# A dynamic convolution feeding a squared-ReLU FFN: fixed instruction order, FFN matmuls in groups of six chunks, one PSUM ring

## The chip, the cores and the metric

The kernel runs on one core of a Trainium2 chip. The metric is device time in microseconds (us) for one execution, lower is better. Engine names in the profile: PE is the matrix engine, PEld its weight loads, DVE the vector engine, ACT the scalar (activation) engine, POOL the GpSimd engine, SP the engine that only issues DMAs here.

## The reference

Each token has 192 channels in 8 heads of 24, and for each head seven softmax weights. The first stage replaces every channel by the weighted sum of itself and its six predecessors in time; the second is a two-layer FFN with hidden width 2048 and a squared ReLU. There are 8 batches of 4096 tokens.

```python
w = softmax(weight_gen, axis=-1)                  # (8, 4096, 8 heads, 7 taps)
x_pad = concat([zeros((B, 6, 192)), x], axis=1)   # causal
# y[b,s,h,g] = sum_k w[b,s,h,k] * x_pad[b, s+k, h, g]
y = einsum('bshk,bskhg->bshg', w, windows(x_pad)).reshape(B*S, 192)
h = maximum(y @ w_in, 0)                          # w_in  (192, 2048)
out = (h * h) @ w_out                             # w_out (2048, 192)
```

## The kernel before

The 32768 tokens are worked in 64 blocks of `TB = 512`, eight blocks to a batch. All matrix work is in 16-bit floats with 32-bit sums in PSUM.

**Softmax** (`st_wg_load`, `st_softmax`). Per batch: one load of the raw weights into a tile of 128 partitions with 32 rows of time and a halo of 6 (38 rows x 8 heads x 7 taps = 2128 numbers), one `Exp` on ACT, one sum and one reciprocal on DVE, and five multiplications on DVE (L147, four of 448 numbers and one of 336) that write the scaled weights, skewed, into a buffer `v`. That buffer goes to DRAM as `vd`, from which blocks read their rows. The weights of batch b+1 are loaded at the first block of batch b, and their softmax stands in the text at its third block.

**Block preparation.** `st_load(j)` reads the block's rows of `vd` (tile `wr`, through the SP queue) and of `x` (tile `xt`, through the POOL queue, cast to 16 bits). `st_band` (five a block, on DVE) multiplies `wr` by a 0/1 band mask into `bd`, a banded matrix for each head. `st_conv(j)` runs 80 small matmuls `xt`, `bd` into the PSUM tile `yp`: each uses 32 columns of the array, and four such column strips work side by side. `st_y_evac(j)` copies `yp` to the 16-bit tile `y` on DVE (L241).

**FFN.** The hidden width is 16 chunks of 128 and is worked in eight pairs `fp`. The 192 input channels are 128 + 64, so `st_mm1` issues, for a pair, two matmuls with `w_a` over 128 rows (L249) and two with `w_b` over 64 rows (L262); the latter two use the upper and the lower half of the array's rows, side by side. All four have 512 columns and write `h`, a PSUM tile of two banks. `st_relu` (ACT, L273) turns `h` into `t`, `st_sq` (DVE, L279) squares it into `g`. `st_mm2(j, part)` is chunk by chunk of tokens: a part is eight matmuls of 192 columns (L289) for 128 tokens and half of the hidden chunks; after four parts ACT copies the PSUM tile `o` to `o_sb` (L298) and SP writes it out. `st_mm2` works on the block before, so each of the eight slots of block j holds the first product of one pair of block j and eight matmuls of the second product of block j-1.

PSUM has eight banks: one tile `yp` (two banks), two tiles `h` (four), two tiles `o` (one each). The order in which each engine gets its instructions is not the text's: a planner sorts them by its own estimate of costs, with the text order as priority. Each engine then runs its list in order.

Of the kernel before, what the change touches and what calls it, by code (L numbers as in the profile page):

```python
# [6 lines left out]

ROW_TILED = True
# [3 lines left out]
def kernel(  # L12
# [16 lines left out]
    nc = tc.nc  # L29
    f32 = mybir.dt.float32  # L30
# [17 lines left out]
    RH = R + KK - 1  # L48
# [33 lines left out]
    vbuf = [const.tile([P, RH + KK - 1, H, SL], f16, name=f"v{i}") for i in range(2)]  # L82
# [13 lines left out]
    def load_weights():  # L96
        nc.gpsimd.dma_start(out=w_a, in_=moe_w_in[0:P, :])
        nc.gpsimd.dma_start(out=w_b[0:LO, :], in_=moe_w_in[P:D, :])
        if ROW_TILED:
            nc.gpsimd.dma_start(out=w_b[LO:P, :], in_=moe_w_in[P:D, :])  # L100
        else:
            nc.vector.memset(w_b[LO:P, :], 0.0)
        nc.gpsimd.dma_start(out=w_o, in_=moe_w_out.rearrange("(c p) m -> p c m", p=P))


    wg_t, vd_t = {}, {}

    def st_wg_load(b):
        wg = p_wg.tile([P, RH, H, KK], f32, name="wg")
        wg_t[b] = wg  # L110
        base = weight_gen[b, 0:R]
        if b < B - 1:
            src = bass.AP(
                tensor=base.tensor, offset=base.offset,
                ap=[[R * HK, P], [1, RH * HK]],
            )
            nc.sync.dma_start(out=wg.rearrange("p r h k -> p (r h k)"), in_=src)
        else:
            nc.vector.memset(wg[:, R:RH], 0.0)
            nc.sync.dma_start(  # L120
                out=wg[:, 0:R].rearrange("p r h k -> p (r h k)"),
                in_=weight_gen[b].rearrange("(p r) h k -> p (r h k)", p=P),
            )
            src = bass.AP(
                tensor=base.tensor, offset=base.offset + R * HK,
                ap=[[R * HK, P - 1], [1, (KK - 1) * HK]],
            )
            nc.sync.dma_start(
                out=wg[0 : P - 1, R:RH].rearrange("p r h k -> p (r h k)"), in_=src
            )  # L130

    def st_softmax(b):
        wg = wg_t[b]
        v = vbuf[b % 2]
        nc.scalar.activation(out=wg, in_=wg, func=ActF.Exp)  # L135
        ssum = p_sm.tile([P, RH, H], f32, name="ssum")
        nc.vector.tensor_reduce(out=ssum, in_=wg, axis=AxisX, op=AluOp.add)  # L137
        rcp = p_sm.tile([P, RH, H], f32, name="rcp")
        nc.vector.reciprocal(out=rcp, in_=ssum)  # L139
        pp = list(v.ap[0])  # L140
        for i0 in range(0, RH, SL):
            n = min(SL, RH - i0)
            vo = bass.AP(
                tensor=v.tensor, offset=v.offset + i0 * H * SL,
                ap=[pp, [H * SL + 1, n], [SL, H], [H * SL, KK]],
            )
            nc.vector.tensor_tensor(  # L147
                out=vo,
                in0=wg[:, i0 : i0 + n],
                in1=rcp[:, i0 : i0 + n].unsqueeze(-1).broadcast_to((P, n, H, KK)),  # L150
                op=AluOp.mult,
            )
        vd = p_dr.tile([S, H * SL], f16, name="vd")
        vd_t[b] = vd
        nc.sync.dma_start(
            out=vd.rearrange("(p r) c -> p (r c)", p=P),
            in_=v[:, KK - 1 : KK - 1 + R].rearrange("p r h c -> p (r h c)"),
        )
# [56 lines left out]
    def st_conv(j):  # L215
        yp = ps_y.tile([P, 2, TB], f32, name="yp")
# [21 lines left out]
    def st_y_evac(j):  # L238
        y = p_y.tile([P, 2, TB], f16, name="y")
        y_t[j] = y  # L240
        nc.vector.tensor_copy(out=y, in_=yp_t[j])  # L241

    def st_mm1(j, fp):
        y = y_t[j]
        h = ps_h.tile([P, 2, TB], f32, name="h")
        h_t[(j, fp)] = h
        for jj in range(2):
            fc = 2 * fp + jj
            nc.tensor.matmul(  # L249
                out=h[:, jj, :], lhsT=w_a[:, fc * P : (fc + 1) * P], rhs=y[:, 0, :],  # L250
                start=True, stop=False,
            )
            if not ROW_TILED:
                nc.tensor.matmul(
                    out=h[:, jj, :], lhsT=w_b[:, fc * P : (fc + 1) * P], rhs=y[:, 1, :],
                    start=False, stop=True,
                )
        if ROW_TILED:
            for jj in range(2):
# [3 lines left out]
                    out=h[:, jj, :],  # L263
# [11 lines left out]
    def st_sq(j, fp):  # L275
        if fp == 0:
            g_t[j] = p_g.tile([P, NF, TB], f16, name="g")
        t1 = t1_t[(j, fp)]
        nc.vector.tensor_tensor(  # L279
            out=g_t[j][:, 2 * fp : 2 * fp + 2, :], in0=t1, in1=t1, op=AluOp.mult  # L280
        )

    def st_mm2(j, part):
        c, half = part // 2, part % 2
        if part % 4 == 0:
            o_t[(j, c // 2)] = ps_o.tile([P, 2, Dm], f32, name="o")
        o = o_t[(j, c // 2)]
        for fc in range(half * NF // 2, (half + 1) * NF // 2):
            nc.tensor.matmul(  # L289
                out=o[:, c % 2, :],  # L290
                lhsT=g_t[j][:, fc, c * P : (c + 1) * P],
                rhs=w_o[:, fc, :],
                start=(fc == 0), stop=(fc == NF - 1),
            )
        if part % 4 == 3:
            hf = c // 2
            o_sb = p_os.tile([P, 2, Dm], f32, name="o_sb")
            nc.scalar.copy(out=o_sb, in_=o)  # L298
            g0 = j * TB + hf * 2 * P
            nc.sync.dma_start(  # L300
                out=out[g0 : g0 + 2 * P, :].rearrange("(s p) d -> p s d", p=P),
                in_=o_sb,
            )

    with nc.allow_low_precision("fp16 matmul pipeline"):
        st_wg_load(0)
        for v in vbuf:
            nc.vector.memset(v, 0.0)  # L308
# [3 lines left out]
        st_softmax(0)  # L312
        st_load(0)
        load_weights()
        st_load(1)
        st_load(2)
# [4 lines left out]
        for j in range(NBLK + 1):  # L321
            nb = j // NBB + 1
            if j < NBLK and nb < B:
                if j % NBB == 0:
                    st_wg_load(nb)
                if j % NBB == 2:
                    st_softmax(nb)
            if j + 3 < NBLK:
                st_load(j + 3)
            for fp in range(NFP):  # L330
                if j < NBLK:
                    st_mm1(j, fp)
                    st_relu(j, fp)
                if j >= 1:
                    st_mm2(j - 1, fp)
# [38 lines left out]
```

## Time and profile before

| | us |
|---|---|
| median of three runs | 957.94 (957.47 to 959.33) |
| the profiled execution, its own time | 957.37 |
| its span, first to last instruction | 955.7 |
| PE busy / DVE / ACT / POOL | 863.3 / 686.6 / 587.3 / 64.9 |
| mean granted PE clock | 0.975 of full |

The span is cut into 40 slices in the profile's second part (23.9 us each; a digit is a tenth). Matmul durations in the profile are from the first column in to the last result out, so that consecutive ones overlap; the distance between their starts is what they cost in a row. A group's row gives busy time, mean duration of one, and the idle time ahead of it with what ended it.

### The profile page before, as it was taken

The page shows a single profiled execution, that of the slowest core. Times are in us where ns is not written, and L with a number is a line of the kernel's source. Part 1 is how long each engine was busy: PE and PEld are TensorE (multiplying, and loading weights), DVE is VectorE, ACT ScalarE, POOL GpSimd, SP SyncE. Part 2 cuts the span into 40 slices and gives each one's busy share as a digit, 9 for nine tenths or more (in the row PEclk, how much of TensorE's full clock was granted, in tenths as well). Part 3 has the DMA queues.
Part 4 walks back from the last instruction along what each step waited for, and adds up shares of the span by engine and source line. Part 5 has one row for each costly group of instructions (what it writes and reads, how often), then busy time and mean ns, then how long its engine had stood idle before and what let it go on. Part 6 is the DMA issues. An engine that isn't in the chain of part 4 may idle for free.

```text
span 955.7 us, 25454 instructions
## 1 busy us (share of the span) xinstructions
PE 863.3 (90%) x11264; PEld 504.9 (53%) x11264; DVE 686.6 (72%) x955; ACT 587.3 (61%) x649; POOL 64.9 (7%) x98
## 2 busy tenths in 40 slices
PE   0195847799999999999999999999999999999998
PEld 0043423455555555555555555555555555555555
DVE  7799997986666666666676666766667666676653
ACT  2173625467666676666766667666676666766665
POOL 4000000000000000000000000000000000000000
PEclk9998777799999999999999999999999999999999
DMA  9533433233332233332333323333233322333011
GB/s 209 153 51 92 114 76 113 62 66 62 54 62 50 54 62 54 61 51 53 62 54 60 52 52 62 54 60 52 53 62 54 60 49 56 61 55 55 27 34 43
DMA packets 123950, 62.52 MB, mean 65 GB/s; under 512 B 88641, under 2 KB 121536, under 8 KB 122944
## 3 DMA queue, kind: packets, MB, share of 16 engines
q0 software_dynamic: 44480, 17.57, 16.7%
q1 hardware_dynamic: 79360, 43.33, 15.8%
q8 instruction: 88, 1.44, 0.6%
q14 instruction: 22, 0.18, 0.1%
HBM read 49.09 MB, written 29.36 MB: 82 GB/s over the span
## 4 chain that ended last, share of the span: by engine, by line
PE 79%; DVE 16%; DMA 3%; issue 1%; ACT 1%; SPq 0%; ACTq 0%; DVEq 0%
PE o L289 37%; PE h L249 21%; PE h L262 15%; DVE v L147 8%; PE yp L228 6%; DVE g L279 3%; DMA wg<-in_weight_gen_dram 2%; DVE bd L200 2%; DVE rcp L139 1%; DVE ssum L137 1%; DVE y L241 1%; DMA wr<-vd 1%; ACT t L273 0%; DMA vd<-v 0%; ACT wg L135 0%
## 5 line engine op out<-in xcount | busy, mean ns | idle before, releaser
L273 ACT ACTIVATE t<-h 128x1024 f16<-128x1024 f32 x512 | 523.3, 1023 | 303.1 <-PE h L262 283.1
L279 DVE TENSOR_TENSOR g<-t 128x1024 f16<-128x1024 f16 x512 | 353.3, 693 | 245.2 <-ACT t L273 242.6
L289 PE MATMUL o<-w_o,g 128*128 128x192 f16 x4096 | 430.0, 249 | 0.3 <-DVE g L279 0.2
L289 PEld LDWEIGHTS <-g 128*128 128x128 f16 x4096 | 314.9, 98 | 117.0 <-issue 115.8
L249 PE MATMUL h<-y,w_a 128*128 128x512 f16 x1024 | 309.8, 385 | 45.1 <-DVE y L241 39.0
L262 PE MATMUL h<-y,w_b 64*128 64x512 f16 x1024 | 201.3, 390 | 0.0
L200 DVE TENSOR_TENSOR bd<-wr,mask 128x832 f16<-128x832 f16 (+2 forms) x320 | 173.2, 576 | 6.8 <-DMA wr<-vd 6.8
L262 PEld LDWEIGHTS <-w_b 64*128 64x128 f16 x1024 | 48.9, 92 | 221.1 <-issue 221.1
L249 PEld LDWEIGHTS <-w_a 128*128 128x128 f16 x1024 | 88.2, 98 | 54.4 <-DVE y L241 39.6
L228 PE MATMUL yp<-bd,xt 128*32 128x104 f16 (+7 forms) x5120 | 71.4, 210 | 43.0 <-DVE bd L200 43.0
L190 POOL DMA_DIRECT2D xt<-in_x_dram x56 | 47.8, 856 | 710.5 <-PE yp L228 671.9
L228 PEld LDWEIGHTS <-xt 128*32 128x32 f16 (+3 forms) x5120 | 59.6, 93 | 54.1 <-issue 45.1
L241 DVE CAST y<-yp 128x1024 f16<-128x1024 f32 x64 | 79.2, 1237 | 2.5
L147 DVE TENSOR_TENSOR v<-wg,rcp 128x448 f16<-128x448 f32 (+1 forms) x40 | 79.9, 2142 | 0.1
L298 ACT COPY o_sb<-o 128x384 f32<-128x384 f32 x128 | 60.6, 473 | 4.3 <-PE o L289 4.3
L135 ACT ACTIVATE wg<-wg 128x2128 f32<-128x2128 f32 x8 | 15.8, 1978 | 56.8 <-DMA wg<-in_weight_gen_dram 56.8
L137 DVE TENSOR_REDUCE ssum<-wg 128x304 f32<-128x2128 f32 x8 | 18.8, 2346 | 4.7 <-ACT wg L135 4.7
L139 DVE RECIPROCAL rcp<-ssum 128x304 f32<-128x304 f32 x8 | 16.1, 2022 | 0.0
L182 POOL DMA_DIRECT2D xt<-in_x_dram x8 | 4.7, 583 | 103.1 <-PE yp L228 103.1
L188 POOL DMA_DIRECT2D xt<-in_x_dram x8 | 6.0, 748 | 0.0
L308 DVE MEMSET v<- 128x1408 uint32 x2 | 2.5, 1232 | 1.4 <-PEq L358 1.2
L135 ACT ACT_TABLE_LOAD x1 | 1.3, 1283 | 0.8 <-PEq L358 0.8
(12 smaller groups left out, 7.4 us busy)
## 6 DMA issues: line engine op xcount, KB each, us to landing
out_dram<-o_sb SPq DMA_DIRECT2D x128, 192.0 KB, 2.0
xt<-in_x_dram POOLq DMA_DIRECT2D x56, 240.0 KB, 4.0
wg<-in_weight_gen_dram SPq DMA_DIRECT2D x7, 1064.0 KB, 6.0
wr<-vd SPq DMA_DIRECT2D x56, 80.0 KB, 2.1
vd<-v SPq DMA_DIRECT2D x8, 512.0 KB, 2.9
xt<-in_x_dram POOLq DMA_DIRECT2D x8, 192.0 KB, 3.8
wg<-in_weight_gen_dram SPq DMA_DIRECT2D x1, 896.0 KB, 5.5
w_o<-in_moe_w_out_dram POOLq DMA_DIRECT2D x1, 768.0 KB, 12.1
```

Source lines behind the costliest of these rows:

```text
L137: nc.vector.tensor_reduce(out=ssum, in_=wg, axis=AxisX, op=AluOp.add)
L147: nc.vector.tensor_tensor(out=vo, in0=wg[:, i0 : i0 + n], in1=rcp[:, i0 : i0 + n].unsqueeze(-1).broadcast_to((P, n, H, KK)), op=AluOp.mult,)
L190: eng.dma_start(out=dst, in_=rows(src, t0 + BASE, width))
L200: nc.vector.tensor_tensor(out=bd_t[j][:, H * lo : H * hi].rearrange("p (h m c) -> p h m c", h=H, c=SL), in0=wr_t[j][:, i].unsqueeze(2).bro ...
L228: nc.tensor.matmul(out=yp[p0 : p0 + m, ci, lo:hi], lhsT=x_t[j][:, i, 32 * q : 32 * q + m], rhs=bd[:, hb if later else ha, :], start=True, ...
L241: nc.vector.tensor_copy(out=y, in_=yp_t[j])
L249: nc.tensor.matmul(out=h[:, jj, :], lhsT=w_a[:, fc * P : (fc + 1) * P], rhs=y[:, 0, :], start=True, stop=False,)
L262: nc.tensor.matmul(out=h[:, jj, :], lhsT=w_b[r0 : r0 + LO, fc * P : (fc + 1) * P], rhs=y[r0 : r0 + LO, 1, :], start=False, stop=True, tile ...
L273: nc.scalar.activation(out=t1, in_=h_t[(j, fp)], func=ActF.Relu)
L279: nc.vector.tensor_tensor(out=g_t[j][:, 2 * fp : 2 * fp + 2, :], in0=t1, in1=t1, op=AluOp.mult)
L289: nc.tensor.matmul(out=o[:, c % 2, :], lhsT=g_t[j][:, fc, c * P : (c + 1) * P], rhs=w_o[:, fc, :], start=(fc == 0), stop=(fc == NF - 1),)
L298: nc.scalar.copy(out=o_sb, in_=o)
```

## The change

1. **Fixed order.** The whole program stands under `tc.manual_schedule()`: every engine gets its instructions in the order of the text.
2. **Groups.** The eight pairs of a block are worked as `GROUPS = [(0,1,2), (3,4,5), (6,7)]`. `st_mm1(j, fps)` issues all `w_a` matmuls of a group (six, six, four) and then all its `w_b` matmuls. After them PE gets the second product of the group before (of the last group of block j-1 where the group is the first). In the third group the convolution of block j+1 stands between the two.
3. **PSUM.** `h` and `yp` share one ring of three two-bank tiles; `o` is one tile of two banks for a whole block. `st_mm2(j, fps)` goes hidden chunk by hidden chunk, and for each over the four sets of 128 tokens. `g` becomes eight tiles, one for a pair.
4. **Copies.** `yp` to `y` moves from DVE to ACT. `o` to `o_sb` moves from ACT to DVE, once a block (768 numbers) instead of twice (384), with one output DMA a block; it is issued between the first and the second square of the next block.
5. **Softmax.** Batch 0 is cut into four parts of 1024 tokens (tile `wg8`, 14 rows = 784 numbers), the first at the start, the second behind the convolution of block 0, the third and the fourth at the head of blocks 0 and 1. Batches 1 to 7 are loaded whole, batch 1 before the first block and batch b+2 at the seventh block of batch b. The softmax of batch b+1 is worked in five chunks of eight rows (448 numbers, the last 336), one at the end of each of the first five blocks of a batch: `Exp` on ACT, sum and reciprocal on DVE, multiplication on POOL. In batch 0 the multiplications are on POOL too, but for the first of part 0, which stays on DVE. The store to `vd` stands at the sixth block.
6. **Weights.** `w_in` is asked for before the masks are made, `w_out` behind the convolution of block 0.

```diff
-    p_g = ctx.enter_context(tc.tile_pool(name="p_g", bufs=2))
-    p_os = ctx.enter_context(tc.tile_pool(name="p_os", bufs=3))
+    p_g = ctx.enter_context(tc.tile_pool(name="p_g", bufs=8))
+    p_os = ctx.enter_context(tc.tile_pool(name="p_os", bufs=2))
-    ps_y = ctx.enter_context(tc.tile_pool(name="ps_y", bufs=1, space=bass.MemoryType.PSUM))
-    ps_h = ctx.enter_context(tc.tile_pool(name="ps_h", bufs=2, space=bass.MemoryType.PSUM))
-    ps_o = ctx.enter_context(tc.tile_pool(name="ps_o", bufs=2, space=bass.MemoryType.PSUM))
+    ps_h = ctx.enter_context(tc.tile_pool(name="ps_h", bufs=3, space=bass.MemoryType.PSUM))
+    ps_o = ctx.enter_context(tc.tile_pool(name="ps_o", bufs=1, space=bass.MemoryType.PSUM))
...
     def st_conv(j):
-        yp = ps_y.tile([P, 2, TB], f32, name="yp")
+        yp = ps_h.tile([P, 2, TB], f32, name="yp", tag="h")
...
-        nc.vector.tensor_copy(out=y, in_=yp_t[j])
+        nc.scalar.copy(out=y, in_=yp_t[j])
...
+    def st_mm1(j, fps):
         y = y_t[j]
+        for fp in fps:
+            h = ps_h.tile([P, 2, TB], f32, name="h", tag="h")
+            h_t[(j, fp)] = h
+            for jj in range(2):
+                fc = 2 * fp + jj
                 nc.tensor.matmul(
+                    out=h[:, jj, :], lhsT=w_a[:, fc * P : (fc + 1) * P], rhs=y[:, 0, :],
+                    start=True, stop=False,
+                )
+        for fp in fps:
             for jj in range(2):
                 fc = 2 * fp + jj
                 r0 = LO * jj
                 nc.tensor.matmul(
-                    out=h[:, jj, :],
+                    out=h_t[(j, fp)][:, jj, :],
                     lhsT=w_b[r0 : r0 + LO, fc * P : (fc + 1) * P],
                     rhs=y[r0 : r0 + LO, 1, :],
...
+    def st_mm2(j, fps):
+        if fps[0] == 0:
+            o_t[j] = ps_o.tile([P, 2, TB], f32, name="o")
+        o = o_t[j]
+        for fp in fps:
+            for jj in range(2):
+                fc = 2 * fp + jj
+                for c in range(TB // P):
+                    nc.tensor.matmul(
+                        out=o[:, c // 2, (c % 2) * Dm : (c % 2 + 1) * Dm],
+                        lhsT=g_t[(j, fp)][:, jj, c * P : (c + 1) * P],
+                        rhs=w_o[:, fc, :],
+                        start=(fc == 0 and c % 2 == 0), stop=(fc == NF - 1),
+                        skip_group_check=True,
+                    )
+
+    def st_o_evac(j):
+        o_sb = p_os.tile([P, 2, 2 * Dm], f32, name="o_sb")
+        nc.vector.tensor_copy(out=o_sb, in_=o_t[j][:, :, 0 : 2 * Dm])
+        nc.sync.dma_start(
+            out=out[j * TB : (j + 1) * TB, :].rearrange("(c p) d -> p c d", p=P),
+            in_=o_sb.rearrange("p a (b d) -> p (a b) d", b=2),
         )
...
+        whole_part(parts[0], (nc.vector, nc.gpsimd))
         st_load(0)
-        load_weights()
+        for s in parts[2:]:
+            s.load(nc.sync)
         st_load(1)
-        st_load(2)
         for i in range(NT):
             st_band(0, i)
         st_conv(0)
         st_y_evac(0)
...
+        load_w_out()
+        whole_part(parts[1], (nc.gpsimd,))
+        st_load(2)
+        nc.vector.memset(v_big, 0.0)
+        nxt = Softmax(1, 0, R, v_big, new_vd(1)) if B > 1 else None
+        if nxt:
+            nxt.load(nc.sync)
+        before = None
+        for j in range(NBLK):
+            b, jb = j // NBB, j % NBB
+            if j < 2:
+                whole_part(parts[2 + j], (nc.gpsimd,))
+            if jb == 6 and b + 2 < B:
+                after = Softmax(b + 2, 0, R, v_big, new_vd(b + 2))
+                after.load(nc.sync)
+            if nxt and jb == 5:
+                nxt.store(nc.sync)
+            if nxt and jb == 6:
+                nxt = after if b + 2 < B else None
             if j + 3 < NBLK:
                 st_load(j + 3)
+            for gi, fps in enumerate(GROUPS):
+                st_mm1(j, fps)
+                if gi == NG - 1 and j + 1 < NBLK:
+                    st_conv(j + 1)
+                if before:
+                    st_mm2(*before)
+                for fp in fps:
                     st_relu(j, fp)
+                if gi == NG - 1 and j + 1 < NBLK:
+                    st_y_evac(j + 1)
+                if j + 1 < NBLK and gi < 2:
+                    for i in ((0, 1, 2), (3, 4))[gi]:
+                        st_band(j + 1, i)
+                if gi == NG - 1 and nxt and jb < len(nxt.chunks()):
+                    i0 = nxt.chunks()[jb]
+                    nxt.exp(i0)
+                    nxt.total(i0)
+                    nxt.recip(i0)
+                    nxt.scale(i0, nc.gpsimd)
+                for n, fp in enumerate(fps):
                     st_sq(j, fp)
+                    if n == 0 and gi == 0 and j >= 1:
+                        st_o_evac(j - 1)
+                before = (j, fps)
+        st_mm2(*before)
+        st_o_evac(NBLK - 1)
```

Here `whole_part(s, engines)` is `exp`, `total`, `recip`, one `scale` per eight rows on the engines in turn, and `store`.

More of the change, by code (lines that the diff above doesn't have):

```diff
@@ L47 @@
     R = S // P
-    RH = R + KK - 1
+    HALO = KK - 1
     SL = 8
@@ L132, in st_softmax @@
[L132 to L148, printed above, removed]
+        for r0 in (0, LO):
+            nc.gpsimd.dma_start(out=w_b[r0 : r0 + LO, :], in_=moe_w_in[P:D, :])
@@ L275, in st_sq @@
     def st_sq(j, fp):
-        if fp == 0:
-            g_t[j] = p_g.tile([P, NF, TB], f16, name="g")
+        g = p_g.tile([P, 2, TB], f16, name="g")
+        g_t[(j, fp)] = g
         t1 = t1_t[(j, fp)]
-        nc.vector.tensor_tensor(
-            out=g_t[j][:, 2 * fp : 2 * fp + 2, :], in0=t1, in1=t1, op=AluOp.mult
-        )
[L283 to L303, printed above, removed]
```

159 lines of the change are left out of this document (84 added, 75 removed).

## The prediction

> **What bounds the kernel now.** I read the page's engine rows and slices first, then the chain, then the groups.
>
> ```profile
> span 955.7 us, 25454 instructions
> PE 863.3 (90%) x11264; PEld 504.9 (53%) x11264; DVE 686.6 (72%) x955; ACT 587.3 (61%) x649; POOL 64.9 (7%) x98
> PE   0195847799999999999999999999999999999998
> PEclk9998777799999999999999999999999999999999
> PE 79%; DVE 16%; DMA 3%; issue 1%; ACT 1%; SPq 0%; ACTq 0%; DVEq 0%
> L273 ACT ACTIVATE t<-h 128x1024 f16<-128x1024 f32 x512 | 523.3, 1023 | 303.1 <-PE h L262 283.1
> L279 DVE TENSOR_TENSOR g<-t 128x1024 f16<-128x1024 f16 x512 | 353.3, 693 | 245.2 <-ACT t L273 242.6
> L147 DVE TENSOR_TENSOR v<-wg,rcp 128x448 f16<-128x448 f32 (+1 forms) x40 | 79.9, 2142 | 0.1
> ```
>
> Two stages stand out. From the tenth slice on PE is full, ACT waits for PE (283 us) and DVE for ACT (243 us): PE sets the pace. In the first nine slices PE is partly idle, its clock drops with that, and the 16% of the chain that lie on DVE are there. The chain in order of time has both; its last two rows are the next block's convolution and the end's matmuls:
>
> ```profile
> 16.65 17.47 DVE v L147 x9
> 84.31 4.07 DVE v L147 x2
> 212.75 1.02 PE yp L228 x80
> 213.77 0.54 PE h L249 x2
> 214.31 0.32 PE h L262 x2
> 214.63 0.77 PE o L289 x8
> 215.40 0.43 PE h L249 x2
> 215.83 0.32 PE h L262 x2
> 226.04 1.02 PE yp L228 x80
> 930.05 1.02 PE yp L228 x80
> 945.61 6.16 PE o L289 x72
> ```
>
> From 212.75 to 930.05 there are 54 blocks of 13.28 us, all alike: 1.02 + 0.54 + 7 x 0.43 + 8 x 0.32 + 8 x 0.77 = 13.29.
>
> **Where 13.28 us go.** The last row streams 72 second-product matmuls in 6.16 us, the end of the last (some 0.25) included: 0.082 each, so eight take 0.66. In a slot they take 0.77, that is 0.11 more behind the half-array `w_b` pair. The `w_a` pair takes 0.43 behind the second product (both use the whole array) but 0.54 behind the convolution's strips: again 0.11. Two `w_b` run side by side and should take what one 512-column matmul takes, 0.43/2 = 0.215; they take 0.32, once more 0.11. So a change between whole array, halves and strips costs PE 0.11 us. A block has 18: into and out of each of eight `w_b` pairs, into and out of the convolution. That is 2.0 us of 13.28.
>
> **The change part by part.**
>
> *Groups, and the second product one group behind.* Matmul counts and shapes stay. Changes of array use fall to 7: two in each of the first two groups, three in the third (to `w_b`, to the strips, to the whole array). 11 x 0.11 = 1.2 us less: PE alone would need 12.07. What no row shows is one `w_b` pair right behind another. Below: 0.215 each, as within the strips, where 80 small matmuls pass in 1.02. Above: a change's price for each following pair, five in a block, 0.55. I take 0.215: the strips reload in the same way, with no gap. The Trainium skill's page "TensorEngine Tiling (Array Packing)" (Key Properties) says that changing the tiling mode, and not just the tile, drains the engine. By that the pairs stream and the term stays nil; a drain at each pair would add 0.55 where nothing hides it.
>
> *The ring of three.* Three relus of group 1 must free their tiles for group 2 (rows of one slot, and of DVE and ACT with work queued up).
>
> ```profile
> 500.79 0.39 PE L262 MATMUL h<-y,w_b 64*128 64x512 f16 x2
> 501.22 1.02 ACT L273 ACTIVATE t<-h 128x1024 f16<-128x1024 f32 x1 [0.50 <-PE h L262]
> 56.46 1.94 ACT L273 ACTIVATE t<-h 128x1024 f16<-128x1024 f32 x2 [0.31 <-PE h L262]
> 54.65 1.88 DVE L279 TENSOR_TENSOR g<-t 128x1024 f16<-128x1024 f16 x3
> 47.47 3.02 DVE L200 TENSOR_TENSOR bd<-wr,mask 128x768 f16<-128x768 f16 x6
> L241 DVE CAST y<-yp 128x1024 f16<-128x1024 f32 x64 | 79.2, 1237 | 2.5
> ```
>
> A relu starts 0.43 behind its `w_b` pair's start (500.79, 501.22), lasts 1.02, and two in a row are 1.94 - 1.02 = 0.92 apart. From the first `w_a` of a block: six `w_a` 1.29, a change 0.11, so the first pair starts at 1.40, relu 1 at 1.83, and relu 3 ends at 1.83 + 2 x 0.92 + 1.02 = 4.69. PE goes on with three pairs (to 2.05), a change and 16 matmuls of the third group of the block before (to 3.47), four `w_a` of group 2 (to 4.33), and then needs the third tile: it waits about 0.40. At group 3 the relus of group 2 end near 8.6, the convolution needs their last tile near 9.4: no wait. `yp` is then copied by ACT behind the two last relus, from 11.3 to 12.35, and the next block starts at 12.47: the margin is 0.1. ACT's price for this copy lies between 1.02 (the relu's row, same size) and 1.24 (DVE's); by the upper end 0.1 is lost. I take 1.02. The block: 12.07 + 0.40 = 12.47. The old order gives way here: a late `y` has no other PE work behind it.
>
> *Copies on DVE.* A block has 8 squares at (1.88 - 0.69)/2 = 0.60 apart, 5 bands at 3.02/6 = 0.5, and one copy of 768 numbers, (768/1024) x 1.24 = 0.93: 8.2 of 12.47. The copy must be over before the second group's second product, 6.0 into the block, overwrites the one `o`; the last matmul into it is at 3.5, one square comes first: it ends near 4.7. Hidden by 1.3.
>
> *Softmax by chunks.* In 35 blocks (7 batches x 5) ACT has an exp of 448, by the rows below 1978 x 448/2128 = 0.42 to 0.6 with a fixed part, behind the copy of `y`, where ACT idles until the next block's relu 1 (1.83 in). DVE has the sum (2346 x 448/2128 = 0.5) and the reciprocal (2022 x 64/304 = 0.43), queued ahead of the last two squares. These end near 13.85 + 1.2 = 15.1, and PE asks for the last at 12.47 + 2.16 + 0.66 = 15.3. Hidden, with 0.2 to spare.
>
> ```profile
> L135 ACT ACTIVATE wg<-wg 128x2128 f32<-128x2128 f32 x8 | 15.8, 1978 | 56.8 <-DMA wg<-in_weight_gen_dram 56.8
> L137 DVE TENSOR_REDUCE ssum<-wg 128x304 f32<-128x2128 f32 x8 | 18.8, 2346 | 4.7 <-ACT wg L135 4.7
> L139 DVE RECIPROCAL rcp<-ssum 128x304 f32<-128x304 f32 x8 | 16.1, 2022 | 0.0
> L91 POOL TENSOR_SCALAR_AFFINE_SELECT mask<-mask 128x104 f16<-128x104 f16 x3 | 0.7, 271 | 0.0
> L190 POOL DMA_DIRECT2D xt<-in_x_dram x56: 845/847/945, 8.5 to 878.3; - x56
> ```
>
> *The multiplication on POOL.* POOL is 7% busy, so its own length L matters only for what waits: the loads of `x` queue behind it, three blocks ahead of need, and cost nothing. But it starts just as DVE has the last squares and then five bands, all of them reading two SBUF tiles. Where PE sets the pace it can gain nothing, so its least is nil. If it holds up the second of those squares by L, 0.5 of L lies under the first one and 0.4 comes back because the ring's wait vanishes when PE is late; the block grows by L - 0.9. L is between 448 x 2.6 ns = 1.2 us (POOL's select row, 271/104) and above 2.25 (DVE's, 2142 a mean with the smaller form). I take 1.6, nearer to POOL's own row, and that it holds DVE up: 35 x 0.7 = 25 us. The row of `x` loads (845 least, 847 middle) shows that POOL isn't slowed beside DVE, but that work reads no tile. The Trainium skill's "SBUF — State Buffer" (Who interferes with whom) says that a vector instruction with two SBUF inputs and a GpSimd instruction that reads SBUF exclude one another for a whole instruction, whoever comes first. No run here shows it yet; it speaks for the 25 us.
>
> *The start.*
>
> ```profile
> 5.81 1.98 ACT L135 ACTIVATE wg<-wg 128x2128 f32<-128x2128 f32 x1 [3.72 <-DMA wg<-in_weight_gen_dram]
> 34.13 2.65 DMA vd<-v
> 36.80 5.49 DMA wr<-vd
> wr<-vd SPq DMA_DIRECT2D x56, 80.0 KB, 2.1
> out_dram<-o_sb SPq DMA_DIRECT2D x128, 192.0 KB, 2.0
> 43.03 2.54 PE L228 MATMUL yp<-bd,xt 128*32 128x104 f16 x80 [43.03 <-DVE bd L200]
> 42.38 4.04 DVE L200 TENSOR_TENSOR bd<-wr,mask 128x832 f16<-128x832 f16 x8 [6.78 <-DMA wr<-vd]
> 47.61 1.01 PE L249 MATMUL h<-y,w_a 128*128 128x512 f16 x2 [2.04 <-DVE y L241]
> 57.73 0.60 PE L249 MATMUL h<-y,w_a 128*128 128x512 f16 x2
> ```
>
> Now block 0's convolution starts at 43.0, its first product at 47.6, block 1's at 57.7, behind ten multiplications for two batches. After: load of 0.4 MB by 4, exp 0.9, sum 0.9, reciprocal 0.75 (784/2128 of the rows), multiplication 2.2 and POOL's beside it, to 9 or 10; store 2.7, rows back 2.1 to 5.5, bands and convolution 3, copy 1.0: block 0 starts near 20. Then it stalls: SP has the load of part 3 (waiting for the tile that POOL's multiplications of part 1 release) ahead of block 1's `wr`. Part 1's exp is behind the copy of `y`: exp, sum, reciprocal 2.5, two multiplications on POOL 3 to 5, `wr` 2.5, three bands 1.5, and only then the squares of block 0: near 31 the second product starts, and what is left of the block takes 7, more while PE's clock is low. Block 1 starts near 40 (35 to 46).
>
> *Between.* Block 9's convolution is at 212.75; at 13.28 it would have come at 43 + 9 x 13.28 = 162.6. These 50 us are DVE's multiplications (79.9 us) in front of squares and copies. After, batches are spread and POOL has them: gone, down to the block's own price.
>
> *The end.* From the last block's start: no convolution, group 2's product ends at 11.5, the last square at 12.1, eight matmuls behind it to 12.9, copy 1.2, output DMA 2 to 2.5, close 0.7: 17.3.
>
> **The sum.** 40 + 62 x 12.47 + 17.3 = 830; with POOL 855. The profiled run took 957.37 for a span of 955.7, and the median 957.94 is 0.06% over it: 2 more. 857 us.
>
> **The rivals.**
>
> *No hold-up by POOL.* The 25 us fall away: 832. For it: POOL's steady 847 ns beside DVE. 26%.
>
> *Slower, by the same multiplication.* L decides. Block growth L - 0.9 in 35 blocks eats the gain of 957 - 832 = 125 us at L = 4.5. DVE itself, at 2.2 for 448 numbers, is slow at this scattered write (the sum reads 2128 in 2.35). If POOL takes twice DVE's time, L = 4.5: 957, and above it slower, 975 at L = 5. The Trainium skill's "GPSIMD Engine Reference" (3.1) gives 1.96 for GpSimd over the vector engine in a two-input operation; taken as a ratio to this row it lands on no gain. Against it: POOL's select goes at 2.6 ns a number. 8% for no gain or slower.
>
> *Only the early gain.* The fixed order loses in new waits (no planner fills them, and `y`, `o` and the ring have margins of 0.1, 1.3 and -0.4) what the seven changes save: 40 + 62 x 13.28 + 17 + 2 = 883. 14%.
>
> *Pairs drain.* Five times 0.11 in a block, of which the ring's wait takes back half: 0.3 x 62 = 19 on top: 876. 8%.
>
> **How the numbers follow.** 44% for the forecast (838 to 880, L from 1.2 to 2.25), with the four above 100%. The range 825 to 905 leaves out the best cases of the first rival and L above 3. A change of 0.2% (2 us) is about what a measurement of this kernel can tell. Faster 0.92, same 0.01, slower 0.07.
>
> **What would show it.** Block starts of PE 12.4 to 12.5 apart in the last three blocks of a batch, and 0.3 to 1.4 more in the first five; `w_b` pairs 0.215 apart; a wait of PE for ACT of 0.4 ahead of the sixth `w_a` of group 2; squares that start late or last longer while POOL multiplies; first `w_a` near 20 us, a gap of about 8 in block 0. Wrong: POOL's multiplication above 3 us, waits of PE for DVE's squares in every block, or a clock below full.

## The result, and the profile after

The changed kernel takes 880.76 us (median; 879.93 to 882.27) against 957.73 (957.47 to 959.33) for the kernel before on the same chip: a ratio of 0.9195, interval 0.9179 to 0.9211. The profiled execution took 880.54 for a span of 878.8. The forecast was 857 with a range of 825 to 905; the measured time lies in that range, and 0.8 above the upper end of the forecast's own band (838 to 880).

From the page of the kernel after:

```profile
span 878.8 us, 25261 instructions
...
PE 796.8 (91%) x11264; PEld 520.6 (59%) x11264; DVE 638.2 (73%) x979; ACT 568.2 (65%) x616; POOL 147.6 (17%) x140
...
PE   0678999989998999998999899998999899999997
...
PEclk9889999999999999999999999999999999999999
...
PE 45%; DVE 24%; ACT 14%; issue 13%; DMA 2%; POOL 1%; ACTq 0%; SPq 0%; DVEq 0%; POOLq 0%
...
L299 DVE TENSOR_TENSOR g<-t 128x1024 f16<-128x1024 f16 x512 | 383.1, 775 | 102.1 <-ACT t L293 102.1
L310 PE MATMUL o<-w_o,g 128*128 128x192 f16 x4096 | 380.5, 248 | 47.8 <-DVE g L299 41.6
```

The weak stretch at the start is down from nine slices to four. After it the 9s are broken by an 8 about every five slices (22 us each), one for each batch of eight blocks. The chain has 24% on DVE where it had 16%, and PE's second product now waits 41.6 us for the squares `g`; their mean rose from 693 to 775 ns.

Starts of the first `w_a` of each block give the whole account. Block 0 starts at 25.29, block 1 at 48.05, block 2 at 68.30. From there the batches run alike: the second to the fifth block of each take 13.55 to 13.63, the sixth 12.74, the other three 12.50. (A chunk of the softmax stands at the end of the first five blocks, so it meets the first squares of the next.) The last batch, with no softmax beside it, has 12.50 throughout; the last block starts at 861.28, and the end is 17.5 behind it.

One block of 12.50, from the timeline of the kernel after (start, length, engine, line, operation; in brackets the idle time before it and what ended it):

```profile
823.78 1.46 PE L274 MATMUL h<-y,w_a 128*128 128x512 f16 x6
...
825.17 0.82 PE L282 MATMUL h<-y,w_b 64*128 64x512 f16 x6
...
825.92 1.49 PE L310 MATMUL o<-w_o,g 128*128 128x192 f16 x16
...
827.25 1.03 PE L274 MATMUL h<-y,w_a 128*128 128x512 f16 x4
...
828.51 0.59 PE L274 MATMUL h<-y,w_a 128*128 128x512 f16 x2 [0.23 <-ACT t L293]
...
836.28 1.03 PE L274 MATMUL h<-y,w_a 128*128 128x512 f16 x4
```

Six `w_a` and one change of array use take 825.17 - 823.78 = 1.39, that is 6 x 0.215 + 0.10. Three `w_b` pairs and a change take 0.75 = 3 x 0.215 + 0.11. Sixteen matmuls and no change take 1.33 = 16 x 0.083. Then four `w_a`, which need 0.86, take 1.26: the third tile of the ring comes 0.40 late (0.23 of it is shown as idle, since matmul records reach past their place in the row).

The same stretch of a block with a softmax chunk (same kernel, same view):

```profile
486.36 1.46 PE L274 MATMUL h<-y,w_a 128*128 128x512 f16 x6
...
487.72 2.72 DVE L299 TENSOR_TENSOR g<-t 128x1024 f16<-128x1024 f16 x2
...
487.99 2.43 POOL L160 TENSOR_TENSOR v_big<-wg,rcp 128x448 f16<-128x448 f32 x1 [10.65 <-DVE rcp L152]
...
488.51 0.83 PE L310 MATMUL o<-w_o,g 128*128 128x192 f16 x8
...
490.50 0.83 PE L310 MATMUL o<-w_o,g 128*128 128x192 f16 x8 [1.16 <-DVE g L299]
...
491.17 1.46 PE L274 MATMUL h<-y,w_a 128*128 128x512 f16 x6
...
492.56 0.82 PE L282 MATMUL h<-y,w_b 64*128 64x512 f16 x6
...
493.43 2.14 PE L310 MATMUL o<-w_o,g 128*128 128x192 f16 x24
...
499.92 1.46 PE L274 MATMUL h<-y,w_a 128*128 128x512 f16 x6
```

Two squares that take 1.28 alone take 2.72 while POOL multiplies; this lengthening is called a hold below. PE waits for the second. Its `w_a` of group 2 starts 4.81 into the block instead of 3.47, and it then passes the ring without its wait.

The start (same kernel, same view):

```profile
6.83 2.15 DVE L160 TENSOR_TENSOR v_small<-wg,rcp 128x448 f16<-128x448 f32 x1
6.93 1.69 POOL L92 TENSOR_SCALAR_AFFINE_SELECT mask<-mask 128x96 f16<-128x96 f16 x1
...
14.33 17.77 SPq L124 DMA_DIRECT2D wg<-in_weight_gen_dram  x2
...
25.29 2.72 PE L274 MATMUL h<-y,w_a 128*128 128x512 f16 x6 [1.11 <-ACT y L264]
...
28.03 3.71 POOL L160 TENSOR_TENSOR v_small<-wg,rcp 128x448 f16<-128x448 f32 x2 [13.93 <-issue]
...
29.27 0.91 DVE L146 TENSOR_REDUCE ssum<-wg 128x112 f32<-128x784 f32 x1
...
32.15 0.43 SPq L213 DMA_DIRECT2D wr<-vd  x1
...
37.10 1.56 DVE L223 TENSOR_TENSOR bd<-wr,mask 128x832 f16<-128x832 f16 x3 [5.96 <-DMA wr<-vd]
...
39.32 4.02 PE L310 MATMUL o<-w_o,g 128*128 128x192 f16 x24 [6.48 <-DVE g L299]
...
53.88 3.98 DVE L223 TENSOR_TENSOR bd<-wr,mask 128x832 f16<-128x832 f16 x3
54.09 3.87 POOL L160 TENSOR_TENSOR v_small<-wg,rcp 128x448 f16<-128x448 f32 x2 [2.00 <-DVE rcp L152]
...
59.38 4.00 PE L310 MATMUL o<-w_o,g 128*128 128x192 f16 x24 [4.32 <-DVE o_sb L320]
```

SP's issue of the loads of parts 2 and 3 lasts from 14.33 to 32.10, because part 3 waits for its tile. Block 1's `wr` goes out only at 32.15, its bands start at 37.10, and the squares of block 0 stand behind them on DVE: PE waits 6.48. In block 1 three bands take 3.98, held by POOL. The copy of `o` queued behind them is late, and PE waits 4.32 for it. After both of these waits PE is also slower for a while: the 24 matmuls behind them take 4.02 and 4.00, where 24 take 2.14 in the block above, and the granted clock in these two stretches is 0.50 (39.3 to 43.3 and 59.3 to 63.4).

### The profile page after: what moved, and what is told of

Its sections match the earlier page's. It is cut to its first block, busy times and chain, and to the rows that moved or that the text cites. A ratio compares the mean times of both kernels' runs of the same rounds, so it can differ in the third digit from the quotient of the medians.

```text
span 878.8 us, 25261 instructions
## 1 busy us (share of the span) xinstructions
PE 796.8 (91%) x11264; PEld 520.6 (59%) x11264; DVE 638.2 (73%) x979; ACT 568.2 (65%) x616; POOL 147.6 (17%) x140
## 4 chain that ended last, share of the span: by engine, by line
PE 45%; DVE 24%; ACT 14%; issue 13%; DMA 2%; POOL 1%; ACTq 0%; SPq 0%; DVEq 0%; POOLq 0%
PE o L310 23%; PE h L274 12%; DVE g L299 9%; ACT t L293 8%; DVE bd L223 7%; PE h L282 7%; ACT y L264 4%; DVE o_sb L320 4%; PE yp L251 3%; DVE ssum L146 3%; DVE rcp L152 2%; ACT wg L139 2%; DMA wr<-vd 1%; POOL mask L92 0%; DMA vd<-v_small 0%
## 5 line engine op out<-in xcount | busy, mean ns | idle before, releaser
L293 ACT ACTIVATE t<-h 128x1024 f16<-128x1024 f32 x512 | 489.8, 1023 | 282.3 <-PE h L282 264.9
L299 DVE TENSOR_TENSOR g<-t 128x1024 f16<-128x1024 f16 x512 | 383.1, 775 | 102.1 <-ACT t L293 102.1
L310 PE MATMUL o<-w_o,g 128*128 128x192 f16 x4096 | 380.5, 248 | 47.8 <-DVE g L299 41.6
L274 PE MATMUL h<-y,w_a 128*128 128x512 f16 x1024 | 259.7, 382 | 8.1 <-ACT t L293 6.9
L160 POOL TENSOR_TENSOR v_big<-wg,rcp 128x448 f16<-128x448 f32 (+1 forms) x35 | 81.6, 2330 | 474.2 <-DVE rcp L152 474.2
L282 PE MATMUL h<-y,w_b 64*128 64x512 f16 x1024 | 144.5, 381 | 0.0
L146 DVE TENSOR_REDUCE ssum<-wg 128x64 f32<-128x448 f32 (+2 forms) x39 | 24.7, 633 | 110.0 <-ACT wg L139 110.0
L251 PE MATMUL yp<-bd,xt 128*32 128x104 f16 (+7 forms) x5120 | 71.1, 210 | 21.6 <-DVE bd L223 21.6
L264 ACT CAST y<-yp 128x1024 f16<-128x1024 f32 x64 | 65.1, 1018 | 19.3 <-PE yp L251 19.3
L320 DVE COPY o_sb<-o 128x768 f32<-128x768 f32 x64 | 60.8, 950 | 3.9 <-PE o L310 1.0
L139 ACT ACTIVATE wg<-wg 128x448 f32<-128x448 f32 (+2 forms) x39 | 23.6, 610 | 2.0 <-DMA wg<-in_weight_gen_dram 2.0
```

The source lines that it names most:

```text
L146: nc.vector.tensor_reduce(out=self.ssum[:, i], in_=self.wg[:, i], axis=AxisX, op=AluOp.add)
L160: eng.tensor_tensor(out=bass.AP(tensor=v.tensor, offset=v.offset + i0 * H * SL, ap=[list(v.ap[0]), [H * SL + 1, n], [SL, H], [H * SL, KK]] ...
L251: nc.tensor.matmul(out=yp[p0 : p0 + m, ci, lo:hi], lhsT=x_t[j][:, i, 32 * q : 32 * q + m], rhs=bd[:, hb if later else ha, :], start=True, ...
L264: nc.scalar.copy(out=y, in_=yp_t[j])
L274: nc.tensor.matmul(out=h[:, jj, :], lhsT=w_a[:, fc * P : (fc + 1) * P], rhs=y[:, 0, :], start=True, stop=False,)
L282: nc.tensor.matmul(out=h_t[(j, fp)][:, jj, :], lhsT=w_b[r0 : r0 + LO, fc * P : (fc + 1) * P], rhs=y[r0 : r0 + LO, 1, :], start=False, stop ...
```

## The experiments

Times are medians; the ratio is to the kernel before on the same chip. The reference point is the changed kernel at 880.76. "Softmax block" means one whose first squares meet POOL's multiplication.

### Is it the multiplication, and is it the reading?

POOL writes the same rows for as long with five memsets (`fill`), and reads nothing. This kernel leaves out the convolution weights of batches 1 to 7:

```diff
-                    nxt.scale(i0, nc.gpsimd)
+                    nxt.fill(i0, nc.gpsimd)
```

> POOL's multiplication of batches 1 to 7 is replaced by five fills of the same rows with zeros, which read no SBUF tile (so the convolution weights of these batches are left out). Sum, reciprocal and exp stay. Theory (a POOL instruction that reads SBUF holds DVE's two-input instructions for its own length): no square lasts above 0.7 us, the first five blocks of a batch fall from 13.55 to 12.5, the time falls by 7 x 4.45 = 31 us to about 850. Rival (exp, sum and reciprocal ahead of the last two squares make them late, POOL has no part in it): blocks stay at 13.55 and the time at 881.

848.49 us, ratio 0.8856 (0.8843 to 0.8869). All blocks from block 2 on take 12.50. The squares by the tile view of this kernel (least/middle/greatest ns), and POOL's writes by its groups:

```profile
L304 DVE TENSOR_TENSOR g<-t x512: 627/685/694, 40.6 to 842.3; 128x1024 f16<-128x1024 f16 x171
```

```profile
L173 POOL MEMSET v_big<- 128x512 f16 (+1 forms) x175 | 88.7, 507 | 8.1
```

and the squares of the changed kernel, by the same view:

```profile
L299 DVE TENSOR_TENSOR g<-t x512: 627/682/2181, 38.6 to 872.6; 128x1024 f16<-128x1024 f16 x171
```

POOL is busy for five memsets of 0.507 in each chunk, 2.5 us, as long as the multiplication's record, and no square is longer than 0.694. Exp, sum and reciprocal are all still there and cost nothing. So the 32 us are the multiplication's hold on the squares, and these memsets have none. (They also write in another pattern, in a row instead of scattered. No run here tells the reading from that.)

### The chunk behind the squares

```diff
+                for n, fp in enumerate(fps):
+                    st_sq(j, fp)
+                    ...
                 if gi == NG - 1 and nxt and jb < len(nxt.chunks()):
                     ...
-                for n, fp in enumerate(fps):
-                    st_sq(j, fp)
-                    ...
```

> The softmax chunk is queued behind the two last squares of the block instead of ahead of them; nothing else changes. Theory (DVE is held by POOL wherever it is): the squares of the third group are out of it, but POOL's 2.4 us now hold the first bands of the next block, and behind these come a square and the copy of o, which PE needs 6.0 into the block: 0.5 to 0.9 us lost in a block instead of 1.05, 865 to 880 us. Rival (only the order of sum and reciprocal ahead of the squares matters): 12.5 in every block, 850 us.

846.42 us, ratio 0.8833 (0.8819 to 0.8846). All blocks from block 2 on take 12.50. From this kernel's timeline, and its bands by the tile view:

```profile
491.11 3.00 DVE L223 TENSOR_TENSOR bd<-wr,mask 128x832 f16<-128x832 f16 x3
...
491.38 2.35 POOL L160 TENSOR_TENSOR v_big<-wg,rcp 128x448 f16<-128x448 f32 x1 [9.68 <-DVE rcp L152]
```

```profile
L223 DVE TENSOR_TENSOR bd<-wr,mask x320: 527/553/2094, 17.5 to 821.0; 128x832 f16<-128x832 f16 x64, 128x768 f16<-128x768 f16 x64, 128x896 f16<-128x896 f16 x32
```

The hold is as strong as before, but it falls on the bands, three of which take 3.00 instead of 1.55, and PE does not wait for them. The whole price is gone with one move of a few lines. The theory had the hold right and its cost at this place (0.5 to 0.9 a block) wrong: it is nil. The rival's 12.5 came, but not for its reason: in the run with memsets the sum and the reciprocal were still ahead of the squares, and the blocks took 12.50 too.

### The start: `wr` of block 1 ahead of the part loads

```diff
         st_load(0)
+        st_load(1)
         for s in parts[2:]:
             s.load(nc.sync)
-        st_load(1)
```

> The loads of block 1 are issued ahead of the loads of parts 2 and 3 on SP. Theory (block 0 stalls because SP waits for part 3's tile with block 1's load behind it): the load is issued near 14.5 instead of 32.2 us, bands of block 1 start near 31 behind the sums of two parts, instead of 37.1, and the time falls by about 6 us, to 875. Rival (DVE and POOL with the parts of batch 0 set this, not the load): within 1 us of 881.

878.45 us, ratio 0.9166 (0.9152 to 0.918). Block 1 starts at 46.3 instead of 48.0. From this kernel's timeline:

```profile
31.59 4.84 DVE L223 TENSOR_TENSOR bd<-wr,mask 128x832 f16<-128x832 f16 x3
```

The bands of block 1 now start at 31.59 instead of 37.10, and run into POOL's multiplications of parts 1 and 2: 4.84 instead of 1.56. The SP queue was a real wait; behind it POOL's hold was next. About 2 us are won, not 6.

Moving the part multiplications out of the way as well (with the chunk behind the squares):

```diff
-            if j < 2:
-                whole_part(parts[2 + j], (nc.gpsimd,))
+            if j in (1, 2):
+                whole_part(parts[1 + j], (nc.gpsimd,))
```

> The squares-first kernel with block 1's loads ahead of the loads of parts 2 and 3, and with parts 2 and 3 one block later (at the head of blocks 1 and 2). Theory (the start is long because POOL's multiplications hold block 1's bands, and the load comes late): the bands of block 1 wait for part 1's multiplications alone, block 0 ends near 43 instead of 48 us, 840 to 842 in all. Rival (the loads of the first rows and the PE clock set the start): 845 or above.

849.77 us, ratio 0.8865 (0.8851 to 0.888): 3.4 more than without this and the early load, and in the range of the rival. Block 1 starts at 41.1 (forecast: near 43), but blocks 1 and 2 take 21.6 and 16.9. From this kernel's timeline:

```profile
28.67 5.34 POOL L160 TENSOR_TENSOR v_small<-wg,rcp 128x448 f16<-128x448 f32 x2 [14.64 <-issue]
29.91 4.00 DVE L223 TENSOR_TENSOR bd<-wr,mask 128x832 f16<-128x832 f16 x3
```

Block 1 did start earlier, as the theory has it, but the total didn't follow: the cost moved with the work to blocks 1 and 2. At 28.67 POOL is delayed as well: two pieces that take it 3.71 in the kernel after take 5.34 here, with the bands beside them. But the first band (29.91) takes only 0.53 in the middle of POOL's first piece (28.67 to 32.50), so these records don't show which of the two waited when.

### What the groups save: changes of array use

Groups of one pair, the product one group behind:

```diff
-    GROUPS = [(0, 1, 2), (3, 4, 5), (6, 7)]
+    GROUPS = [(i,) for i in range(NFP)]
```

> Eight groups of one pair instead of 3, 3 and 2: 18 changes of array use in a block as before, in the fixed order. Theory (each change costs PE 0.11 us): 12.1 + 11 x 0.11 = 13.3 us for a block without softmax, and up to 0.45 more because only eight matmuls of the second product stand between the convolution and the need of its copy y: 13.3 to 13.75, total 930 to 960. Rival (the gain of the blocks came from the order and not from the changes): 12.5 a block, 881.

1205.37 us, ratio 1.2581 (1.256 to 1.2602): both expectations missed. From the groups of this kernel:

```profile
L310 PE MATMUL o<-w_o,g 128*128 128x192 f16 x4096 | 449.5, 255 | 227.3 <-DVE o_sb L320 131.4 <-DVE g L299 90.7
```

One pair leaves a slot of some 1.5 us (0.43 + 0.32 + 0.77) for a relu of 1.02, a square of 0.69 and what lies between them. That is too short, and the copy of `o` stands behind a late square: the second product waits for both, and the plain blocks take 15.82. The run says nothing on changes of array use.

The same with the product three groups behind, the copy of `o` moved to the third group, the convolution behind the seventh, and the chunk behind the squares:

```diff
-                if before:
-                    st_mm2(*before)
+                if len(before) == 3:
+                    st_mm2(*before.pop(0))
```

> Squares ahead of the softmax chunk as in the squares-first kernel; groups of one pair, but the second product three groups behind and the convolution behind the seventh group, so that neither squares nor y are late. 17 changes of array use in a block instead of 7, no wait for the ring. Theory (a change costs PE 0.11 us): 12.07 + 10 x 0.11 = 13.2 us a block, 846 + 62 x 0.7 = 890 us. Rival (it was the distance to the second product, not the changes): 12.1 to 12.5, 825 to 846 us.

1054.65 us, ratio 1.1007 (1.0989 to 1.1026). The total missed, because softmax blocks grew to 15.4 to 18.8. The plain blocks, 13.54, answer the question; from this kernel's timeline, one wait in them:

```profile
1012.08 0.39 PE L282 MATMUL h<-y,w_b 64*128 64x512 f16 x2
...
1012.78 0.82 PE L310 MATMUL o<-w_o,g 128*128 128x192 f16 x8 [0.31 <-DVE o_sb L320]
```

The product starts 0.70 behind the start of its `w_b` pair where it takes 0.32 without a wait, so the wait costs 0.38 (as with the ring, the idle time shown is less). Without it 13.16 with 17 changes; the changed kernel without its ring wait, 12.50 - 0.40 = 12.10 with 7. The difference is 1.06 for ten changes, 0.11 each, the figure the prediction read from the rows of before.

Groups of two, two, three and one, so that the ring never has to turn within a group (with the chunk behind the squares):

```diff
-    GROUPS = [(0, 1, 2), (3, 4, 5), (6, 7)]
+    GROUPS = [(0, 1), (2, 3), (4, 5, 6), (7,)]
```

> Squares first as before, groups of 2, 2, 3 and 1 pairs: 9 changes instead of 7, and PE has 16 matmuls of the second product between a group's relus and the need of their tiles, and 24 while y is copied. Theory (0.4 us of a block are the ring's wait): 12.07 + 2 x 0.11 = 12.3 us a block without a wait, 833 us. Rival (the wait is not the price, or y or the squares get late with shorter groups): 12.5 or more, 846 us or above.

900.41 us, ratio 0.9398 (0.9384 to 0.9412). Plain blocks take 12.71, softmax blocks 13.95. From this kernel's timeline:

```profile
503.62 1.48 PE L310 MATMUL o<-w_o,g 128*128 128x192 f16 x16 [1.57 <-DVE o_sb L320]
...
860.58 1.48 PE L310 MATMUL o<-w_o,g 128*128 128x192 f16 x16 [0.33 <-DVE o_sb L320]
```

The ring's wait is gone, and one for the copy of `o` stands in its place, 0.33 in a plain block and 1.57 where held bands come ahead of the copy. So the copy first, and the bands behind the squares:

```diff
+                if gi == 0 and j >= 1:
+                    st_o_evac(j - 1)
+                for fp in fps:
+                    st_sq(j, fp)
                 if j + 1 < NBLK and gi < 2:
                     for i in ((0, 1, 2), (3, 4))[gi]:
                         st_band(j + 1, i)
...
```

> The squares-first kernel with groups of 2, 2, 3 and 1 pairs, the copy of o ahead of the squares of the first group, and the bands behind the squares. Theory (9 changes and no ring's wait make 12.3 us where no softmax chunk is; in the others POOL holds the first squares, which PE needs 3.7 us into the block, by 0.4): 12.3 and 12.75 us, 840 to 850 in all. Rival (12.5 is what ACT and DVE allow, whatever the groups): 12.5 or more in the blocks without softmax.

853.95 us, ratio 0.8906 (0.8893 to 0.8919). All blocks from block 2 on take 12.64, softmax or not. From this kernel's timeline:

```profile
788.41 1.49 PE L310 MATMUL o<-w_o,g 128*128 128x192 f16 x16 [0.25 <-DVE g L299]
```

PE no longer waits for the copy, but for the squares behind it, and the time is above the 840 to 850 of the theory. The rival's 12.5 or more came. Three groups of six chunks with a ring wait of 0.40 (12.50) remain better than four groups without one.

### What the fixed order does by itself

The changed text under the planner:

```diff
-    with nc.allow_low_precision("fp16 matmul pipeline"), tc.manual_schedule():
+    with nc.allow_low_precision("fp16 matmul pipeline"):
```

> The changed kernel with the planner's order instead of the order of the text; all else as changed. Theory (the fixed order only keeps what the text says; groups and ring make the block): blocks of 12.5 to 13.3 us where the planner keeps groups together, 860 to 930 in all. Rival (the order itself is the gain of the steady blocks): 13.3 or more in the blocks without softmax, over 930.

885.72 us, ratio 0.9246 (0.9232 to 0.9259). From this kernel's page:

```profile
PE   0567649999999999999999999999999999999997
...
POOL 8966870000000000000000000000000000000000
```

The planner moves all of POOL's multiplications to the first six slices. Blocks 0 to 4 take 19.0, 22.7, 25.9, 30.0 and 14.1, and every later one 12.50. So the plain blocks go from 13.28 to 12.50 without the fixed order. The planner's blocks 0 to 4 lose 49 us over 12.50 each, the fixed order's blocks 0 and 1 lose 18 and its later blocks 30 in holds. That leaves 1, and the planner's first product comes 3.7 later (29.01): together the 5 us between the two. With the chunk behind the squares it is 39 shorter than the planner's.

The other way round, the kernel before with its multiplication (L147) on POOL:

```diff
-            nc.vector.tensor_tensor(
+            nc.gpsimd.tensor_tensor(
```

> The kernel before with one edit: the multiplications of the softmax on POOL instead of DVE, order by the planner. Theory (the 50 us lost in its first nine blocks are DVE's 80 us of multiplications): the start is 4 us later since POOL takes 2.4 us where DVE starts one each 1.9, and 25 to 45 us of the rest go: 915 to 935. Rival (DVE is held by POOL for as long as it would have worked itself, or the planner's order and not the engine makes the loss): within 10 us of 958.

948.75 us, ratio 0.9907 (0.9893 to 0.9922). From this kernel's page:

```profile
PE   0385657999999999999999999999999999999998
```

The rival's forecast for the total came (within 10 of 958), and the theory's for the start did not: the first product comes at 41.71, 5.9 earlier than before (47.61) and not 4 later. That is most of the 9 us won. Of the 50 us lost in the early blocks only 3 come back: blocks 2, 3 and 4 take 26.9, 26.1 and 32.3, and block 6 takes 15.3. Squares last up to 2.20 here too (0.69 in the middle). Under the planner's order the engine alone changes little; the kernels above, with the same multiplication on POOL, differ by when it is done.

### The copies, and a version that beats both

The chunk behind the squares, `y` copied by DVE and `o` by ACT as in the kernel before:

```diff
-        nc.scalar.copy(out=y, in_=yp_t[j])
+        nc.vector.tensor_copy(out=y, in_=yp_t[j])
...
-        nc.vector.tensor_copy(out=o_sb, in_=o_t[j][:, :, 0 : 2 * Dm])
+        nc.scalar.copy(out=o_sb, in_=o_t[j][:, :, 0 : 2 * Dm])
```

> The squares-first kernel with the two copies back on their old engines: y on DVE, o on ACT, in the same places. Theory (both copies lie under PE's work on either engine): blocks of 12.5 us, 844 to 850. Rival (DVE needs the relief): y is late behind the squares or the bands, 0.2 us a block or more, 858 or above.

844.40 us (843.74 to 845.21), ratio 0.8809 (0.8796 to 0.8822). The blocks stay at 12.50, so the exchange of copies brings nothing to the steady part. Block 1 takes 14.60 instead of 16.89: the copy of `o` no longer stands behind held bands.

To this, `w_out` asked for right behind `w_in`:

```diff
         load_w_in()
+        load_w_out()
...
-        load_w_out()
```

> The kernel with the copies swapped back, and the load of the second weight matrix (768 KB) right behind those of the first instead of ahead of the first rows' return. Theory (block 0 begins 5 us later than forecast because the rows of the weights come back behind that load: 7.6 us from issue to use, where the DMA engines are over 0.9 busy from 13 to 22 us): block 0's first product at 21 to 23 instead of 25 us, 840 to 843 in all. Rival (the return waits for its own many small pieces, whatever else is loaded, or the other loads fill the gap): 844 or above.

842.29 us (841.16 to 842.75), ratio 0.8788 (0.8776 to 0.88), the shortest of all, though its interval still touches that of the kernel without this edit. The longest early pieces of its chain of waits, and its first product by the timeline:

```profile
14.83 3.11 DMA wr<-vd
28.52 5.12 DMA wr<-vd
```

```profile
22.54 2.72 PE L274 MATMUL h<-y,w_a 128*128 128x512 f16 x6 [1.33 <-DVE y L264]
```

The same pieces in the kernel after, by its chain:

```profile
13.80 7.60 DMA wr<-vd
32.15 4.93 DMA wr<-vd
```

In the kernel after, block 0's rows travel beside the load of `w_out`, asked for at 12.89, and come back in 7.60; in the swapped-back kernel, which differs from this one only by that load's place, it is 7.32. With the load done earlier it is 3.11, and the first product comes at 22.54 instead of 25.13. Block 0 is 0.8 shorter too, and block 1 gives 1.7 back: it takes 16.27 instead of 14.60. Block 1's own rows take as long as before (5.12).

## Why the prediction was right, and where it was off

| step of the prediction | forecast | measured |
|---|---|---|
| first `w_a` | near 20 | 25.29 |
| second product of block 0 | near 31 | 39.32 |
| block 1 starts | 40 (35 to 46) | 48.05 |
| block without softmax | 12.47 | 12.50 |
| ring of three, wait in group 2 | 0.40 | 0.40 |
| change of array use | 0.11 | 0.10 to 0.11; 0.11 by groups of one |
| `w_b` pairs | 0.215 | 0.215 |
| hold by POOL | 35 x 0.7 = 25 | 28 x 1.05 + 7 x 0.24 = 31 |
| block 1 itself | as the others | 20.26, 6.7 over a softmax block |
| end behind the last block's start | 17.3 | 17.5 |
| span | 855 | 878.8 |

The profiled span forecast by the same sum is 855. The 24 us between it and 878.8 are 8.0 (start of block 1) + 6.7 (block 1) + 6.6 (POOL, against 35 x 0.7 = 24.5) + 62 x 0.03 = 1.9 + 0.2 (end), and some 0.5 in blocks of 13.6.

**Right.** The steady block, by its parts. The Trainium skill's "TensorEngine Tiling (Array Packing)" (Key Properties) says that a change of tiling mode drains the engine, and the trace agrees: 0.11 at each change, none from one pair to the next. The two rivals nearest the measured time, pairs that drain (876) and only the early gain (883), are refuted by their own marks: pairs stream, and blocks take 12.50 and not 13.28. That the number fell between them is chance. No hold-up by POOL (832) is refuted by the squares of 2.18; even without the hold, with the chunk behind the squares, the time is 846, because of the start. The copies and the softmax operations of ACT and DVE were hidden in the blocks as forecast: with all of them in place and memsets on POOL, blocks take 12.50.

**The term L.** The prediction let the hold be L, with 0.5 of it under the first square and 0.4 given back by the ring. In the softmax block above, the second square lasts 2.17, and 0.68 is the middle of all squares: the hold lengthens it by 1.5. The second product would go on at 489.17 (488.51 + 8 x 0.083) and goes on at 490.50, 1.33 later. Of this 0.40 come back as the ring's wait, and 0.12 are added at the next group, whose product starts 0.87 behind its `w_b` (492.56 to 493.43) instead of 0.75, right behind the late copy of `o` (492.44 to 493.38). That is 1.33 - 0.40 + 0.12 = 1.05. The chunk of 336 numbers cost 0.24.

So the mechanism was right and the size too small (0.7 where 1.05 was measured); that it came so near is luck. L = 1.6 rested on the 2.6 ns of POOL's select, but the multiplication's record is 2.20 when nothing holds it and 2.43 here, and either of them in the formula gives 1.3 or 1.5 a block. The record is longer than the hold, as the tile view of the part multiplications in the kernel after shows, two at a time in stretches of 3.71 and 3.70:

```profile
L160 POOL TENSOR_TENSOR v_small<-wg,rcp x4: 1900/2056/2205, 28.0 to 34.1; 128x448 f16<-128x448 f32 x2, 128x336 f16<-128x336 f32 x2
```

Of 3.70 the second piece (1.90) leaves 1.80: so long after the first it starts, though the first's record is 2.20. What a held instruction gains is 1.5 both times it was seen by itself: squares 2.18 against 0.68, bands 2.09 against 0.55. The rule of "SBUF — State Buffer" (Who interferes with whom) in the Trainium skill, that an instruction with two SBUF inputs on DVE and one on POOL that reads SBUF exclude each other, agrees with these rows: squares and bands are held, memsets on POOL hold nothing, and DVE's sum with its one input (0.91 at 29.27 beside POOL, 0.97 at 26.03 without it) is not held. That it is a whole instruction that excludes the other is not shown: the hold is shorter than the record, and one band passed inside it (29.91 in the kernel with the part multiplications moved).

**The slower rival's price.** Twice DVE's time did not come: 2.20 on POOL when it is not held, 2.15 on DVE for the same 448 numbers. The ratio 1.96 of the Trainium skill's "GPSIMD Engine Reference" (3.1) does not hold for this scattered write, and the measurement decides.

**The start was the largest miss**, 14.7 us with block 1, and block 1's start (48.05) lies outside its own range of 35 to 46. "Rows back 2.1 to 5.5" was 7.60 beside `w_out`. "2.5" for block 1's `wr` was 4.93; no run shows what made it long. The hold by POOL, priced in the steady blocks, was not carried over to the bands that DVE works in block 1, where two multiplications stand in a row and the copy of `o` behind the bands. And PE's clock of 0.50 after the two waits cost about 2 us in each of blocks 0 and 1. The early-load and start experiments show that the load and the part multiplications, moved one at a time, each uncover the next wait.

## What to carry to other kernels

Moving work to an idle engine need not be free: here POOL's multiplication held DVE's two-input operations. Look at what the other engine has in its queue at that moment, and put the work where the held operation has slack. Here one move of a few lines was worth 34 us, nearly half of what the whole change brought. Price a start by its own chain with every DMA that is in flight beside it; rows that landed in 2.1 (median before) or 3.0 (median after) took 4.93 and 7.60 there.

## What the runs showed of the hardware that was not expected

- POOL is delayed as well: its mask select takes 0.27 alone and 1.69 beside DVE's multiplication (at 6.93), and its two multiplications stretch from 3.71 to 5.34 where three bands run beside them.
- A multiplication's record on POOL is longer than its place in the row: 2.20 against 1.80 when another follows.
- Block 0's rows came back in 3.11 or in 7.60, depending on when one other load (`w_out`, asked for 0.9 us ahead of them in the slow case) was under way.
